# Moving the last batch's router chain, the row statistics and a hold on raw weights in a fused attention and mixture-of-experts kernel

## Chip, cores and metric

The kernel runs on one core of one Trainium2 chip. The metric is the device time of one execution in microseconds (us); lower is better. Engines are called as in the profile: PE (TensorE matmul, with PEld for its weight loads), DVE (VectorE), ACT (ScalarE), POOL (GpSimd) and SP (SyncE, which here only issues DMAs).

## What is computed

Causal attention with a cumulative bias (8 batches, 8 heads, 576 positions, head size 64), then a mixture of experts over the 4608 resulting rows of 512: each row goes to the one expert whose embedding it resembles most, passes through that expert's two layers and is scaled by the softmax weight of its choice.

```python
scores = scale * np.matmul(q, k.transpose(0, 1, 3, 2))
cum = np.cumsum(np.maximum(s, 0.0), axis=-1)
bias = -(cum[:, :, :, None] - cum[:, :, None, :])
scores = np.where(causal, -1000000000.0, scores + np.minimum(bias, 0.0))
...
out = np.matmul(attn, v)
...
logits = xn @ en.T / tau
expert_idx = np.argmax(logits, axis=1)
gate_w = probs[np.arange(N), expert_idx]
for e in range(E):
    mask = expert_idx == e
    h = np.maximum(x[mask] @ w1[e], 0.0)
    out[mask] = gate_w[mask, None] * (h @ w2[e])
```

## The kernel before, in words

The program is one instruction stream per engine, and its order is written out by hand (the schedule is manual): each engine takes its instructions in the order in which the program emits them, and waits at the head of its queue. So what sets the time around the change is who stands behind whom in a queue.

Attention runs head by head (`step(n)`, 64 heads). When the last head of a batch is normalised (`norm1` to `norm3`, which write the batch's rows into `xt`), `router` appends a chain of small tasks for that batch's 576 rows: `sume` (logits per expert, DVE), `sel1` to `sel5` (the largest one, as a one-hot `oh`), `rank0` (ten small PE matmuls that count rows per expert), `rank1` to `rank3` (DVE: the place `pos` of each row in its expert's list), and five scatters `scat` (indirect DMAs issued on POOL) that write the rows to the DRAM table `xs`. For the last batch, `rows` follows, which makes the indices of all later gathers. `chain(k)`, `slot`, `mslot` and `some` are the places at which the program takes tasks from this chain.

The experts run one after the other. Rows of an expert are gathered from `xs` by POOL in tiles of 128 (`xload(e, t)`, into one of three slots of `Qx`), transposed on PE (`xtr`), split into a high and a low half-precision part (`xcv`: high by ACT, low by DVE), and their statistics are taken (`xstat`: sum of squares by ACT, three small DVE operations). `gate` makes the row weights of them. Layer 1 (`l1`, line 903) computes for each of eight column blocks m twelve matmuls: four parts c times three products (high x high, high x low of the rows, low of the weights x high). ACT writes the high half of the result, DVE the low half (lines 909 and 910, called evacuation below). Layer 2 is `l2m` (line 974).

Expert 0 begins before its list is complete: while the last heads still run, its first 256 rows go through layer 1 (`first_pass(m)`, "pass m", between and after the last heads' `pv`), then its rows 256 to 383 (the third pass, `l1(m, 0, SPL, SPM)`), which need only the rows of earlier batches. Its row tiles 3 and 4 need the last batch's scatters: these are gathered by `xload(0, 3)` and `xload(0, 4)` and transposed in `third` and `fourth`, in the middle of layer 2 of tiles 1 and 2. `fifth` does row tile 2 of expert 1.

Weights come raw from DRAM through a ring of 14 places (`wissue`, DMAs of 128x512 floats on SP; tile number q counts them, 16 per expert), are squared and summed by ACT (`wsq`), scaled (`wparts`), and split: ACT writes the high half (`wcv`), DVE the low half (`wlow`, line 883, called low half below). When the low half of tile q is written, tile q + 15 is among those that may be issued; the DMA waits on SP for the place's last reader. Tiles 16 to 23 are layer 1 of expert 1, 24 to 31 its layer 2.

Around the change, after the last `pv`, one piece of the chain stands at a time between passes 1 to 7; `rank0` stands behind pass 5, `rank1` behind pass 7, `rank2`, `rank3`, `rows` and the scatters behind the third pass's first block, the low halves and statistics of row tiles 0 to 2 behind the whole third pass:

```python
first_pass(5)
some(0)
...
for m in range(8):
    l1(m, 0, SPL, SPM)
    if m == 0:
        some(4)
wlow(4)
classes()
for t in range(3):
    xstat(0, t)
    if t < 2:
        xload(0, t + 3)
```

Of the kernel before, what the change touches and what calls it, by code (L numbers as in the profile page):

```python
# [114 lines left out]
def main(ctx, tc, qkh, qkc, vtin, s_in, emb, tau, w1h, w2h, out, shared, nb):  # L115
# [573 lines left out]
    X, WT, HT = {}, {}, {}  # L689
# [80 lines left out]
    def xcv(e, t):  # L770
        pv = X[("p", e, t)].rearrange("p (c t) -> p c t", c=4)
        xH = X[("H", e)][:, :, 128 * t:128 * t + 128]
        nc.scalar.copy(xH, pv)
        xL = X[("L", e)]
        if isinstance(xL, tuple):
            xL = xL[e + t // (SPL // 128) > 0]
        nc.vector.tensor_tensor(xL[:, :, 128 * t:128 * t + 128], pv, xH, op=ALU.subtract)
# [102 lines left out]
    def wlow(k=99):  # L880
        for _ in range(min(k, len(lows))):
            q, l, a, s, h = lows.popleft()
            nc.vector.scalar_tensor_tensor(l, a, s, h, op0=ALU.mult, op1=ALU.subtract)  # L883
            wissue(q + 15)
# [6 lines left out]
    def l1(m, e, lo, hi, mid=None):  # L891
# [9 lines left out]
        for c in range(4):  # L901
            for k, (w, x) in enumerate(((wH, xH), (wH, xL), (wL, xH))):
                nc.tensor.matmul(h, w[:, 128 * c:128 * c + 128], x[:, c, lo:hi], start=(c == 0 and k == 0), stop=(c == 3 and k == 2))  # L903
                if m >= a0:
                    nc.tensor.matmul(X["a"][:, HALF * m:HALF * m + HALF], w[:, 128 * c:128 * c + 128], x[:, c, hi:hi + HALF], start=(c == 0 and k == 0), stop=(c == 3 and k == 2))  # L905
            if c == 1 and mid:
                mid()
# [279 lines left out]
    def step(n):  # L1187
# [43 lines left out]
        if n < NH:  # L1231
            wlow(1)
# [168 lines left out]
    for f in (norm1, norm2, norm3):  # L1401
        f(NH - 1)
        wn.pop(0)()
    wlow(1)
    first_pass(1)
    wn.pop(0)()
    chain(1)
    wn.pop(0)()
    wcv(2, True)
    first_pass(2)  # L1410
    chain(1)
    wlow(1)
    chain(2)
    wcv(2, True)
    first_pass(3)
    wcv(2, True)
    chain(1)
    wlow(1)
    chain(2)
    first_pass(4)  # L1420
# [3 lines left out]
    xcv(0, 2)  # L1424
    first_pass(5)
    some(0)
    wlow(1)
    wcv(1, True)
    xinfo(0, NF, NTL)
    first_pass(6)  # L1430
    wlow(1)
    wcv(1, True)
    first_pass(7)
    chain(1)
    wlow(1)
    wcv(1, True)
    for m in range(8):
        l1(m, 0, SPL, SPM)
        if m == 0:
            some(4)  # L1440
            assert not (mq or tasks or first or late or scats)
    wlow(4)
    classes()
    for t in range(3):
        xstat(0, t)
        if t < 2:
            xload(0, t + 3)
    for f in X[("g", 0, 0)][0:2]:
        f()
    xinfo(1, 0, NTL)  # L1450
    xload(1, 2)
# [254 lines left out]
```

## Time and profile before

| | |
|---|---|
| median of 3 runs | 764.95 us (763.99 to 767.49) |
| profiled execution | 763.98 us |
| its span, first to last instruction | 762.3 us |
| mean granted PE clock | 0.995 of full speed |
| PE, DVE, ACT, POOL busy | 97%, 70%, 75%, 52% of the span |

Times inside the profile count from the span's start. A row of the timeline gives the start, the duration, the engine, the line, what is written from what, and in brackets how long the engine stood idle before it and who ended that. Durations of matmuls overlap: the step from one start to the next is what one costs. The granted clock of PE is given in shares of full speed. Time that an engine other than PE stands idle costs nothing in itself.

### The profile page before, as it was taken

Reading aid. Unit: us, or ns where it says so; the run is one execution under the profiler, and the core shown is the slowest. Engines: PE = TensorE matmul, PEld = TensorE weight load, DVE = VectorE, ACT = ScalarE, POOL = GpSimd, SP = SyncE. Lnnn points to the kernel's source line nnn. Section 1 sums busy time; section 2 is a strip of 40 time slices with the busy share of each in tenths; the row PEclk is TensorE's granted clock in tenths of the full one; section 3 lists DMA queues with packets and bytes.
Section 4 is the critical chain, followed back from the end, with each engine's and each line's share of the span. In section 5 each row is a group of like instructions: output and inputs, shape, how many; then the busy total and the mean of one; then the engine's idle time right before and its main releaser. Section 6 shows DMA issues by size and latency. Waiting matters only on the chain. (4 is left out here: it accounts for less than half of the span.)

```text
span 762.3 us, 20951 instructions
## 1 busy us (share of the span) xinstructions
PE 739.1 (97%) x7992; PEld 536.4 (70%) x7992; DVE 530.2 (70%) x1818; ACT 568.2 (75%) x1029; POOL 397.2 (52%) x376
## 2 busy tenths in 40 slices
PE   7999999999999999999689999999999999999996
PEld 4889999999999999998365455545444554554554
DVE  8778888888888888898467767655665566745621
ACT  9898989898989998986377867837648578475410
POOL 9997898989897989693422113222221122312011
PEclk9999999999999999999899999999999999999999
DMA  7789879797979796874525956845755668553001
GB/s 151 175 193 191 173 180 204 180 207 168 216 172 210 181 215 155 174 256 132 172 89 168 207 171 194 159 139 152 181 171 141 177 186 186 169 130 100 13 15 58
DMA packets 76003, 124.01 MB, mean 163 GB/s; under 512 B 38824, under 2 KB 39232, under 8 KB 75033
## 3 DMA queue, kind: packets, MB, share of 16 engines
q0 software_dynamic: 19632, 69.69, 39.4%
q1 hardware_dynamic: 56260, 52.84, 25.9%
q8 instruction: 71, 1.16, 0.7%
q14 instruction: 40, 0.32, 0.1%
HBM read 93.99 MB, written 21.49 MB: 151 GB/s over the span
## 5 line engine op out<-in xcount | busy, mean ns | idle before, releaser
L252 POOL TENSOR_TENSOR PL<-P 128x576 f16<-128x576 f32 (+2 forms) x128 | 205.6, 1726 | 13.1 <-ACT P L498 8.6
L903 PE MATMUL pe<-xH,wt 128*128 128x512 f16 (+1 forms) x576 | 153.1, 344 | 0.5 <-PEq L1008 0.5
L982 POOL DMA_INDIRECT out<-Kx,xj x39 | 43.2, 1108 | 195.0 <-DVE Kx L981 164.5
L903 PEld LDWEIGHTS <-wt 128*128 128x128 f16 x960 | 86.0, 98 | 80.8 <-issue 1.5
L526 PE MATMUL om<-vh,P 128*128 128x73 f16 x960 | 106.9, 199 | 0.5 <-DVE sc L1035 0.3
L528 PE MATMUL om<-vh,PL 128*128 128x73 f16 x960 | 106.1, 197 | 0.9 <-POOL PL L252 0.9
L527 PE MATMUL om<-vl,P 128*128 128x72 f16 x960 | 106.3, 196 | 0.0
L739 POOL DMA_INDIRECT Qx<-xs,idx x40 | 46.5, 1163 | 108.3 <-ACT vjunk L838 41.3
L362 PE MATMUL s<-qkb 96*128 96x288 f32 (+4 forms) x272 | 96.2, 368 | 2.0 <-DVE M L370 0.9
L903 PE MATMUL pe<-xL,wt 128*128 128x512 f16 (+1 forms) x288 | 96.0, 344 | 0.0
L527 PEld LDWEIGHTS <-P 128*128 128x128 bf16 x960 | 94.7, 99 | 0.9 <-issue 0.5
L528 PEld LDWEIGHTS <-PL 128*128 128x128 f16 x960 | 93.8, 98 | 1.0 <-POOL PL L252 1.0
L526 PEld LDWEIGHTS <-P 128*128 128x128 bf16 x960 | 93.8, 99 | 0.6 <-DVE xt L551 0.4
L905 PE MATMUL pxs<-xH,wt 128*128 128x64 f16 x432 | 83.2, 193 | 0.0
L370 DVE CUSTOM_DVE_ANT_0 junk<-s,mS 128x448 bf16<-128x448 f32 (+3 forms) x144 | 73.9, 520 | 5.0 <-PE s L362 3.1
L974 PE MATMUL pxs<-wt,hq 128*128 128x512 f16 x297 | 74.0, 384 | 0.0
L501 ACT ACTIVATE P<-tb 128x1024 f32<-128x1024 f32 x64 | 65.2, 1018 | 3.0 <-PE tb L467 1.9
L974 PEld LDWEIGHTS <-hq 128*128 128x128 f16 x360 | 35.5, 99 | 42.7 <-issue 1.7
L905 PEld LDWEIGHTS <-wt 128*128 128x128 f16 x648 | 63.5, 98 | 0.4
L464 PE MATMUL tb<-QC,KC 128*128 128x448 f32 (+3 forms) x256 | 63.4, 307 | 0.0
L460 PE MATMUL tb<-qkb 128*128 128x448 f32 (+3 forms) x256 | 61.1, 286 | 0.0
L883 DVE SCALAR_TENSOR_TENSOR wt<-ring,idx,wt 128x512 f16<-128x512 f32 x80 | 56.8, 745 | 4.7 <-ACT wt L875 4.6
(328 smaller groups left out, 1997.3 us busy)
## 6 DMA issues: line engine op xcount, KB each, us to landing
qkb<-qkh POOLq DMA_DIRECT2D x15, 1216.0 KB, 8.9
ring<-w2h SPq DMA_DIRECT2D x44, 256.0 KB
ring<-w1h SPq DMA_DIRECT2D x36, 256.0 KB
KC<-qkh POOLq DMA_DIRECT2D x14, 576.0 KB, 8.5
QC<-qkh POOLq DMA_DIRECT2D x14, 576.0 KB, 9.1
vT<-vtin SPq DMA_DIRECT2D x24, 320.0 KB
rw<-w1h SPq DMA_DIRECT2D x15, 256.0 KB
rw<-w2h SPq DMA_DIRECT2D x12, 256.0 KB
```

The source lines that it names most:

```text
L252: nc.gpsimd.tensor_tensor(out, a, b_, op=ALU.subtract)
L362: nc.tensor.matmul(out, G[g]["QB"][0:96, h, 128 * i:128 * i + 128], G[g]["KB"][0:96, h, lo:hi], start=True, stop=True)
L370: nc.vector.tensor_tensor_reduce(out=jk, in0=src, in1=ms, scale=1.0, scalar=NEG, op0=ALU.add, op1=ALU.max, accum_out=MP[n // 2][:, n % 2, ...
L460: nc.tensor.matmul(out, G[g]["KB"][:, h, ks:ks + 128], G[g]["QB"][:, h, 64 + qlo:64 + qhi], start=start, stop=False)
L464: nc.tensor.matmul(out, HD[n]["KC"][:, ks:ks + 128], HD[n]["QC"][:, qlo:qhi], start=False, stop=stop)
L501: nc.scalar.activation(HD[n]["P32"][:, 576:1600], HD[n]["tb"], AF.Exp, scale=0.125)
L526: nc.tensor.matmul(out, lh, vh[:, kb], start=(kb == 0), stop=False)
L527: nc.tensor.matmul(out[:, u:u + 72], lh, vl[:, kb], start=False, stop=False)
L528: nc.tensor.matmul(out, ll, vh[:, kb], start=False, stop=(kb == j))
L903: nc.tensor.matmul(h, w[:, 128 * c:128 * c + 128], x[:, c, lo:hi], start=(c == 0 and k == 0), stop=(c == 3 and k == 2))
L905: nc.tensor.matmul(X["a"][:, HALF * m:HALF * m + HALF], w[:, 128 * c:128 * c + 128], x[:, c, hi:hi + HALF], start=(c == 0 and k == 0), sto ...
L974: nc.tensor.matmul(y, h, w, start=(m == 0 and k == 0), stop=(m == 7 and k == 2))
```

## The change

It moves work; no arithmetic is added but one memset of a single element. Four parts:

- The last batch's chain follows its rows at once: `sume` before pass 1, `sel1` to `sel5` in turn with the weight scaling behind pass 1, `rank0` inside pass 4 (behind its ninth matmul), `rank1` to `rank3` and the scatters behind pass 4. `rows` stands behind pass 6. High halves of weights (`wcv`) and the transposes of row tile 2 shift by a pass to make room, and one low half leaves the last head's step.
- Row statistics of tiles 0, 1 and 2 stand behind pass 7 and inside the third pass (behind blocks 1 and 4), each followed by the gather that takes its slot. Four low halves stand in the third pass as well.
- The order of matmuls inside `l1` for expert 0's first 256 rows and the first block of the third pass: products that need late operands come last.
- Raw weights from tile 22 on are held (`X["hold"]`) until a memset on POOL, behind the three gathers, has written into ring place 0; SP's DMA of tile 22 waits for it.

```diff
-    X, WT, HT = {}, {}, {}
+    X, WT, HT = {"hold": 22}, {}, {}
...
     def xcv(e, t):
+        xch(e, t)
+        xcl(e, t)
...
-            wissue(q + 15)
+            wissue(min(q + 15, X.get("hold", 16 * NE)))
...
-        for c in range(4):
-            for k, (w, x) in enumerate(((wH, xH), (wH, xL), (wL, xH))):
-                nc.tensor.matmul(h, w[:, 128 * c:128 * c + 128], x[:, c, lo:hi], start=(c == 0 and k == 0), stop=(c == 3 and k == 2))
...
-            if c == 1 and mid:
+        ps = [(wH, xH), (wH, xL), (wL, xH)]
+        if e == m == 0 and lo < SPM:
+            cs = [(c, p) for p in (ps[0], ps[2], ps[1]) for c in range(4)]
+        elif e + lo == 0:
+            cs = [(c, p) for c in range(4) for p in ps[0:2]] + [(c, ps[2]) for c in range(4)]
+        else:
+            cs = [(c, p) for c in range(4) for p in ps]
+        for i, (c, (w, x)) in enumerate(cs):
+            nc.tensor.matmul(h, w[:, 128 * c:128 * c + 128], x[:, c, lo:hi], start=(i == 0), stop=(i == 11))
...
+            if i == 8 and mid:
                 mid()
...
-        if n < NH:
+        if n < NH - 1:
             wlow(1)
...
     for f in (norm1, norm2, norm3):
         f(NH - 1)
-        wn.pop(0)()
-    wlow(1)
-    first_pass(1)
-    wn.pop(0)()
-    chain(1)
-    wn.pop(0)()
+    wlow(1)
+    chain(1)
+    first_pass(1)
+    for _ in range(5):
+        wn.pop(0)()
+        chain(1)
+    chain(1)
     wcv(2, True)
     first_pass(2)
-    chain(1)
-    wlow(1)
-    chain(2)
     wcv(2, True)
-    first_pass(3)
-    wcv(2, True)
-    chain(1)
     wlow(1)
-    chain(2)
-    first_pass(4)
+    first_pass(3)
+    l1(4, 0, 0, SPL, mslot)
+    chain(4)
+    some(0)
+    wcv(2, True)
+    wlow(1)
+    wcv(1, True)
+    first_pass(5)
     wlow(1)
     wcv(1, True)
     xtr(0, 2, pxs())
-    xcv(0, 2)
-    first_pass(5)
-    some(0)
-    wlow(1)
+    xch(0, 2)
+    first_pass(6)
+    xcl(0, 2)
+    chain(1)
     wcv(1, True)
     xinfo(0, NF, NTL)
-    first_pass(6)
-    wlow(1)
-    wcv(1, True)
     first_pass(7)
-    chain(1)
-    wlow(1)
+    xstat(0, 0)
+    xload(0, 3)
     wcv(1, True)
     for m in range(8):
         l1(m, 0, SPL, SPM)
         if m == 0:
-            some(4)
...
+        if m == 1:
+            xstat(0, 1)
+            xload(0, 4)
+        if m in (2, 3, 5, 6):
+            wlow(1)
+        if m == 4:
+            xstat(0, 2)
+            xinfo(1, 0, NTL)
+            xload(1, 2)
+            X.pop("hold")
+            nc.gpsimd.memset(HT["ring"][0:1, 0:1], 0.0)
+    wissue(14 + wdone[0] - len(lows))
     wlow(4)
...
     classes()
-    for t in range(3):
-        xstat(0, t)
-        if t < 2:
-            xload(0, t + 3)
-    for f in X[("g", 0, 0)][0:2]:
-        f()
-    xinfo(1, 0, NTL)
-    xload(1, 2)
```

`xch` and `xcl` are the two halves of the former `xcv`. The first two parts of `gate` run between `wlow(4)` and `classes()` now.

Order of DVE from the evacuations of passes 5 and 6 to the places, before (line 639 is `rank1`, 651 the end of `rank3` that writes `pos`, 910 an evacuation, 883 a weight low half, 777 the low part of row tile 2):

```order
L777 TENSOR_TENSOR xL<-pxs,xH 128x4x128
L910 SCALAR_TENSOR_TENSOR hq<-pxs,hq 128x256
L883 SCALAR_TENSOR_TENSOR wt<-ring,idx,wt 128x512
L910 SCALAR_TENSOR_TENSOR hv<-h,hv 128x256
L883 SCALAR_TENSOR_TENSOR wt<-ring,idx,wt 128x512
L910 SCALAR_TENSOR_TENSOR hv<-pxs,hv 128x256
L639 TENSOR_TENSOR idx<-om,base 128x40
L641 TENSOR_TENSOR base<-base,om 128x8
L883 SCALAR_TENSOR_TENSOR wt<-ring,idx,wt 128x512
L910 SCALAR_TENSOR_TENSOR hp<-pe,hp 128x128
L647 TENSOR_TENSOR idx<-idx,oh 128x40
L651 TENSOR_REDUCE pos<-idx 128x5
```

And in the change, from the choice (line 623, `oh`) to the places (922 is the evacuation, 889 the low half):

```order
L623 TENSOR_TENSOR oh<-wsel,idx 128x40
L922 SCALAR_TENSOR_TENSOR hq<-h,hq 128x256
L889 SCALAR_TENSOR_TENSOR wt<-wt,idx 128x512
L922 SCALAR_TENSOR_TENSOR hp<-pxs,hp 128x256
L922 SCALAR_TENSOR_TENSOR hq<-h,hq 128x256
L639 TENSOR_TENSOR idx<-om,base 128x40
L641 TENSOR_TENSOR base<-base,om 128x8
L647 TENSOR_TENSOR idx<-idx,oh 128x40
L651 TENSOR_REDUCE pos<-idx 128x5
```

Three evacuations (passes 2, 3 and 4) and one low half stand between choice and places now; the low halves of layer 2's weights and the evacuations of passes 5 to 7 have gone behind the places.

Order of PE at the rank matmuls (lines 630 to 636), in the change, inside pass 4 (line 915 is layer 1; `h` is pass 4's result):

```order
L915 MATMUL h<-rv,wt 128x256
L915 LDWEIGHTS wt
L915 MATMUL h<-xH,wt 128x256
L630 LDWEIGHTS tri
L630 MATMUL om<-oh,tri 128x40
L633 LDWEIGHTS onesb
L633 MATMUL om<-oh,onesb 128x32
```

Before, the same ten matmuls follow the last matmul of pass 5, one and a quarter passes later.

Order of POOL from the last batch's scatters (line 670) on, in the change, with line 739 the gathers and 1461 the memset:

```order
L713 MEMSET hq 128x64
L670 DMA xs<-xt,pos 36864x580 x5
L739 DMA Qx<-xs,idx 128x580 x3
L1461 MEMSET ring 1x1
L739 DMA Qx<-xs,idx 128x580
L994 DMA out<-Kx,xj 4608x512 x2
```

Only the memset is new on POOL; the three gathers ahead of it are tiles 3 and 4 of expert 0 and tile 2 of expert 1. SP's order is unchanged but for the wait of tile 22 on POOL.

## Rows read from the trace of the kernel before

**Rows 1.** The page's first part: busy time, share of the span, instructions, by engine.

```profile
PE 739.1 (97%) x7992; PEld 536.4 (70%) x7992; DVE 530.2 (70%) x1818; ACT 568.2 (75%) x1029; POOL 397.2 (52%) x376
```

**Rows 2.** Waits of PE from 355 to 500: total us, times, longest.

```profile
PE pxm L767 <- DMA Qx<-xs,idx: 5.9, 1, 5.9
PE pxs L767 <- DMA Qx<-xs,idx: 1.8, 1, 1.8
```

**Rows 3.** Timeline of PE around the first wait: start, us, operation, [idle before].

```profile
366.34 1.46 PE L974 MATMUL pxs<-wt,hp 128*128 128x512 f16 x6
367.64 0.81 PE L974 MATMUL pxs<-wt,hq 128*128 128x512 f16 x3
374.39 1.12 PE L767 MATMUL pxm<-ident,Qx 128*128 128x128 f32 x4 [5.94 <-DMA Qx<-xs,idx]
...
376.58 2.77 PE L974 MATMUL pxs<-wt,hq 128*128 128x512 f16 x6
```

**Rows 4.** Windows: us, busy of PE, PEld, DVE, ACT, POOL, PEclk, DMA share, GB/s.

```profile
355.00:361.00 6.00, 6.00 (x103) 5.91 (x102) 4.52 (x18) 3.56 (x11) 1.59 (x2) 1.00 0.49 161
361.00:368.50 7.50, 7.45 (x39) 3.30 (x36) 6.45 (x29) 4.39 (x14) 3.51 (x4) 1.00 0.80 270
368.50:374.40 5.90, 0.01 (x1) 0.01 (x1) 0.34 (x2) 0.00 (x0) 2.85 (x3) 0.86 0.31 104
374.40:380.00 5.60, 5.60 (x17) 2.60 (x18) 1.72 (x5) 2.65 (x7) 1.92 (x3) 0.54 0.43 104
...
395.80:402.00 6.20, 6.20 (x34) 3.35 (x35) 4.49 (x24) 4.82 (x13) 0.33 (x1) 1.00 0.20 59
```

**Rows 5.** Timeline of POOL: the last scatters of two batches, and the gathers behind them.

```profile
344.24 1.20 POOL L670 DMA_INDIRECT xs<-xt,pos  x1 [0.17 <-issue]
347.49 1.04 POOL L739 DMA_INDIRECT Qx<-xs,idx  x1 [2.05 <-DMA xs<-xt,pos]
...
359.10 1.02 POOL L670 DMA_INDIRECT xs<-xt,pos  x1 [10.00 <-DVE hp L910]
...
364.44 0.99 POOL L670 DMA_INDIRECT xs<-xt,pos  x1 [0.30 <-issue]
370.93 1.05 POOL L739 DMA_INDIRECT Qx<-xs,idx  x1 [5.50 <-DMA xs<-xt,pos]
```

**Rows 6.** Timeline of DVE: the last batch's rows, choice and places.

```profile
346.05 0.53 DVE L551 TENSOR_TENSOR xt<-om,z 128x360 f32<-128x360 f32 x1
...
351.43 0.19 DVE L623 TENSOR_TENSOR oh<-wsel,idx 128x40 bf16<-128x40 f32 x1
...
358.15 0.20 DVE L651 TENSOR_REDUCE pos<-idx 128x5 int32<-128x40 f32 x1
```

**Rows 7.** Timeline of PE: first matmul of pass 4, transposes of tile 2, rank matmuls.

```profile
349.35 0.27 PE L903 MATMUL h<-xH,wt 128*128 128x256 f16 x1
...
351.16 0.63 PE L767 MATMUL pxs<-ident,Qx 128*128 128x128 f32 x4 [0.34 <-DMA Qx<-xs,idx]
...
352.93 0.18 PE L630 MATMUL om<-oh,tri 128*128 128x40 bf16 x1
```

**Rows 8.** Timeline of DVE: low halves, and nine small statistics operations up to the reciprocal.

```profile
335.78 3.10 DVE L883 SCALAR_TENSOR_TENSOR wt<-rw,idx,wt 128x512 f16<-128x512 f32 x1
...
361.88 2.73 DVE L883 SCALAR_TENSOR_TENSOR wt<-ring,idx,wt 128x512 f16<-128x512 f32 x4
...
365.00 0.15 DVE L748 SCALAR_TENSOR_TENSOR xj<-Qx,idx 128x1 int32<-128x1 int32 x1
...
365.94 0.17 DVE L102 RECIPROCAL idx<-idx 128x3 f32<-128x3 f32 x1
```

**Rows 9.** Timeline of SP: weight loads beside the last scatters.

```profile
362.70 2.33 SPq L826 DMA_DIRECT2D ring<-w2h  x4
```

**Rows 10.** Timeline of ACT: one square of the row statistics with its read.

```profile
361.54 0.62 ACT L751 ACTIVATE vjunk<-Qx 128x512 bf16<-128x512 f32 x1
362.06 0.19 ACT L751 ACTIVATION_READ_ACCUMULATOR vjunk<-Qx 128x1 f32 x1
```

More of the change, by code (lines that the diff above doesn't have):

```diff
@@ L770, in xcv, with xch, xcl @@
     def xcv(e, t):
+        xch(e, t)
+        xcl(e, t)
+    def xch(e, t):
+        nc.scalar.copy(X[("H", e)][:, :, 128 * t:128 * t + 128], X[("p", e, t)].rearrange("p (c t) -> p c t", c=4))
+    def xcl(e, t):
         pv = X[("p", e, t)].rearrange("p (c t) -> p c t", c=4)
         xH = X[("H", e)][:, :, 128 * t:128 * t + 128]
-        nc.scalar.copy(xH, pv)
         xL = X[("L", e)]
@@ L900, in l1 @@
         h = (pe() if e or lo else pxs() if m % 2 else ps_t.tile([128, 2, 512], F32, tag="t", name="h")[:, 0])[:, 0:hi - lo]
-        for c in range(4):
-            for k, (w, x) in enumerate(((wH, xH), (wH, xL), (wL, xH))):
-                nc.tensor.matmul(h, w[:, 128 * c:128 * c + 128], x[:, c, lo:hi], start=(c == 0 and k == 0), stop=(c == 3 and k == 2))
-                if m >= a0:
-                    nc.tensor.matmul(X["a"][:, HALF * m:HALF * m + HALF], w[:, 128 * c:128 * c + 128], x[:, c, hi:hi + HALF], start=(c == 0 and k == 0), stop=(c == 3 and k == 2))
-            if c == 1 and mid:
+        ps = [(wH, xH), (wH, xL), (wL, xH)]
[7 more added lines that the diff above has]
+            nc.tensor.matmul(h, w[:, 128 * c:128 * c + 128], x[:, c, lo:hi], start=(i == 0), stop=(i == 11))
+            if m >= a0:
+                nc.tensor.matmul(X["a"][:, HALF * m:HALF * m + HALF], w[:, 128 * c:128 * c + 128], x[:, c, hi:hi + HALF], start=(i == 0), stop=(i == 11))
+            if i == 8 and mid:
                 mid()
@@ L1439, in main @@
         if m == 0:
-            some(4)
             assert not (mq or tasks or first or late or scats)
-    wlow(4)
-    classes()
-    for t in range(3):
-        xstat(0, t)
-        if t < 2:
-            xload(0, t + 3)
-    for f in X[("g", 0, 0)][0:2]:
-        f()
-    xinfo(1, 0, NTL)
-    xload(1, 2)
+        if m == 1:
[10 more added lines that the diff above has]
+    wissue(14 + wdone[0] - len(lows))
+    wlow(4)
+    g = X[("g", 0, 0)]
+    g[0]()
+    for i, f in enumerate(g[4]):
+        if i in (2, 5):
+            wlow(1)
+        f()
+    classes()
     def opening():
```

## The prediction, made before the change was run

> **What bounds the kernel now.** The page's first part comes first: TensorE (PE) is busy 97% of the span, VectorE (DVE) 70%, ScalarE (ACT) 75% [rows 1]. So only stretches in which PE stands still, or runs at the low clock, can be won. The list of waits of PE over the change between attention and experts has just two of weight, both for gathers of token rows: 5.9 and 1.8 us [rows 2]. The timeline shows the first: the second tile's output matmuls stop, and the transposes of row tile 3 of expert 0 begin at 374.39 after 5.94 us of nothing, so PE was free at 368.45 [rows 3]. The windows show what follows: after that standstill the granted clock is 0.54 in the stretch 374.4 to 380.0, about the lower of the two levels (1.2 against 2.4 GHz), where the stretches before and those after 395.8 show 1.00 [rows 4]. Six matmuls take 2.77 us there and 1.46 us at full clock [rows 3].
>
> Why that gather is late is read backwards. It was issued at 370.93, 5.50 us after POOL came free, and what ended that wait was the last scatter of rows landing; the five scatters of the last batch went out from 359.10 to 364.44 [rows 5]. The first scatter followed the places (`pos`), which DVE wrote at 358.15. The rows themselves were there at 346.05 + 0.53 = 346.58, and the one-hot choice `oh` at 351.43 [rows 6]. So 11.8 us lie between rows and places, and the work in them is short: what takes the time is the queue order, the rank matmuls standing behind pass 5 (352.93) [rows 7], and DVE's places standing behind weight halves and evacuations.
>
> **The change, part by part.**
>
> *Chain moved up.* DVE now does the row sums at about 347.2 (rows at 346.58, then one weight low half of 0.68, [rows 8]), and then the evacuation of pass 1 and eleven small operations, two chains interleaved. Nine such small operations took 365.94 - 365.00 = 0.94 us [rows 8]; dependent ones go slower, so I take 1.5 us, and `oh` at 349.5 instead of 351.43. The rank matmuls are now after the ninth of the 12 matmuls of pass 4, which starts at 349.35 [rows 7] and lasts 1.3 (its matmuls have half the columns of the 0.22 us ones below): they are due at 350.3, so PE does not wait for `oh`. If it did, the bound is the present time of `oh`, 351.6: 1.3 us. Next on DVE are the evacuation of pass 4 (PE ends it at 350.9, ACT 0.4 later, DVE at 351.8) and the four rank operations, so `pos` is there at 352.5 against 358.35. POOL followed 0.75 later [rows 5, 6]: the first scatter at about 353.2, 5.9 us earlier.
>
> *Scatters and gather.* Five scatters at (364.44 - 359.10) / 4 = 1.33 us: the last at 358.5. From the last scatter's issue to the gather that needs it took 370.93 - 364.44 = 6.5 us here, beside weight loads, and 347.49 - 344.24 = 3.25 us for the batch before [rows 5]. So the gather goes out between 361.8 and 365.0; I take nearer the first, because the loads beside the scatters go. From its issue to the transposes took 374.39 - 370.93 = 3.46 us [rows 3, 5]: rows in place at 365.2 to 368.5. PE wants them at 368.45. The wait of 5.94 us goes whole, or all but 0.1.
>
> *What the weight hold does.* Four loads of 256 KB were issued from 362.70 on [rows 9], where the DMA engines were 0.80 busy [rows 4]. Now tiles 22 to 29 go behind a one-element POOL memset that stands behind three gathers. POOL reaches it three issues of 1.33 after 361.8 to 365.0: at 365.8 to 369. Eight loads, 2.1 MB, at the 270 GB/s of the stretch 361.0 to 368.5 [rows 4] need 7.8 us, so they are in by 374 to 377. ACT asks for the first two of them (squares of tiles 22 and 23) behind the transposes of row tile 4. From 368.45 PE has 24 matmuls to do before those, at (367.64 - 366.34) / 6 = 0.22 [rows 3], and three groups of transposes of 0.6 [rows 7]: ACT asks at about 375.5, and waits 1.5 us at most. PE then has 15 more such matmuls (3.3), and two groups of 12 with a quarter of the columns (0.7 each) before its PSUM buffers are full and it needs ACT again: at about 381, with the branch between. Cost 0; the cover is PE's own work of that stretch. SP has nothing behind these loads that anyone asks for sooner.
>
> *Clock.* With no standstill the stretch 374.4 to 380.0 runs at 1.00: 5.60 x (1 - 0.54) = 2.6 us gained.
>
> *Row statistics in the third pass.* They leave a place where they cost PE nothing: it is busy 7.45 of 7.50 us there [rows 4]. In 355 to 361 DVE is busy 4.52 of 6 us, ACT 3.56 [rows 4]. DVE gets four low halves (2.73 [rows 8]) and three groups of statistics (0.94), and loses two low halves of 0.68 and the rank operations (0.8): 1.5 more, as much as is free. ACT gets three squares of 0.8 [rows 10], 2.4 more, again as much as is free. So both just keep up, and PE waits at most a little, for the late operand half of tile 2 in the first group of the third pass and a PSUM buffer of pass 7. Ends: 0, or the 1.5 in full behind PE. I take 0.4. The pass order that asks for the weights' low half last is the cover on DVE's late low halves; without it pass 6 would wait about 0.5.
>
> *Transposes of tile 2* now come after pass 5 instead of before it, so the 0.34 us they waited [rows 7] goes. The second large wait, 1.8 us, rests on a gather that goes out behind row tile 0 of expert 1 at the same distance as before: unchanged.
>
> *Sum:* -5.9 - 2.6 - 0.3 + 0.4 = -8.4 us. The profiled execution took 763.98 (span 762.3), so 755.6; the median of the three runs, 764.95, is 0.97 above it. On the median: **756.5 us**, -1.1%. About 0.5% (3.8 us) is what a measurement of this kernel can tell from no change.
>
> **A rule that speaks against it.** Scatters are now issued while DVE is densest. In the rows, 364.44 back to 359.10 were issued at even steps of 1.33, three of them while DVE did four low halves of two SBUF inputs in 2.73 us, 0.68 each: neither side slowed [rows 5, 8]. But one low half beside POOL's subtractions took 3.10 us [rows 8]. The Trainium skill, "SBUF — State Buffer", section "Who interferes with whom", has VectorE and GpSimd share a port pair under an exclusive lock, so that descriptors of a DMA issued on GpSimd wait for some VectorE operations. By that, scatters among DVE's copies and tensor_scalar work would come later than I take them (first rival); the trace bears out the lock for POOL's reading work, and for scatters not.
>
> **Rivals.**
> - *Scatters blocked or landing slowly.* As a mechanism of this kernel: if each of the five waited for one DVE operation, at most the 0.68 of a low half, the gather would be 3.4 us later, 365.2 to 368.4, and rows in place at 368.7 to 371.9: a wait of 0.3 to 3.4, up to about 760. For it: 6.5 us from the last scatter to the gather. Against: the even steps. This is also how the Trainium skill's rule of the port pair would show; no row shows a scatter held so. 10%.
> - *The wait only moves.* `oh` or the places come as late as before because DVE is bound, the wait stays above 4 us and the clock drops again: 761 to 764. Against: only small operations stand ahead of them. 4%.
> - *The 1.8 us wait goes as well,* because its gather meets less traffic: 756.5 - 1.8 = 754.7. Against: the moved loads have landed when that gather goes out, as before. 6%.
> - *The hold turns into a wait, and it is slower.* Place: ACT's squares of tiles 22 and 23, with evacuations behind them in its queue. If the eight loads run at the 104 GB/s seen from 368.5 to 380 [rows 4], they need 20 us and end at 386 to 389, against 381 where PE next needs ACT: a wait of 5 to 8, and 2.6 more for the clock. It eats the gain of 8.4 once they land after 387; at 389 the time is 764.95 + 8 + 2.6 - 8.4 = 767. For it: one burst of eight instead of spread loads, beside gathers. Against: 104 GB/s came with no work queued, and 270 with it. 3%.
>
> **How the numbers follow.** Forecast 77%, its own range 754.5 to 758.5 (0 to 1.5 us in the passes, and a median up to 1 us higher or lower, as runs lie). Chances: faster by over 0.5% is the forecast, the third rival and all of the first, with nothing of the rest counted: 0.93. Within 0.5%: 0.06, the second rival and the fourth up to a landing at 391. Slower: 0.01, the fourth beyond that. The range takes in the first and third rival: 753.8 to 760.0.
>
> **What would show it.** Right: in the list of PE's waits the 5.9 us entry for the gather is gone and the 1.8 us one stands; the granted clock is 1.00 from 361 to 400; the first scatter is at 353 to 354 and the gather 361.5 to 365.5; PE in 355 to 361 is without a wait over 0.5. Wrong: PE waits at the rank matmuls or in the third pass; the last scatter still takes over 7 us to release the gather; a wait of ACT on a ring load near 376 with PE standing still behind it; or a new standstill after 381.

## Result, and the profile after

The changed kernel takes 760.4 us (median of seven runs, 757.39 to 762.29). The kernel before, timed beside it, takes 766.47 (seven runs, 763.99 to 768.14). The ratio is 0.9914, with a 95% interval of 0.9897 to 0.993, so the change gains 6.6 us (5.4 to 7.9). The forecast was 756.5, a gain of 8.4. The profiled execution took 760.35 us, with a span of 758.6.

The kernels were timed in four sessions (the expectations say calls): the result; then the first four runs, the next four and the last four. The kernel before had medians of 766.47, 769.78, 766.38 and 769.53 us in them, so a ratio holds only inside its session. In the two sessions near 770 the profiles show PE standstills that have no releaser (such as 2.1 us in six pieces at L941, "<- issue"), and the one kernel that was timed in a session of each kind gained less there. What makes the difference is not shown; the third and the fourth session are both noted for the same chip.

Line numbers are shifted by the diff: of the lines cited, L767 stayed, L883 is L889, L903 is L915, L974 is L986. The waits of PE from 320 to 500 in the changed kernel (total us, times, longest; first three lines) answer to [rows 2]:

```profile
PE pxs L767 <- DMA Qx<-xs,idx: 3.0, 1, 3.0
PE om L526 <- DVE xt L551: 2.0, 1, 2.0
PE V L300 <- DVE vl L311: 0.5, 1, 0.5
```

The 5.9 us entry for `pxm` is gone. Its other gather wait grew from 1.8 to 3.0 us, and a wait of 2.0 for normalised rows (`om <- xt`) stands at 340, ahead of the stretch that the prediction looked at. The timeline of PE shows the three places: the wait at 340, the transposes of row tile 3, and the second gather wait with the six matmuls behind it [rows 3]:

```profile
340.31 0.19 PE L526 MATMUL om<-vh,P 128*128 128x73 f16 x1 [1.97 <-DVE xt L551]
...
370.40 0.60 PE L767 MATMUL pxm<-ident,Qx 128*128 128x128 f32 x4
...
390.36 1.12 PE L767 MATMUL pxs<-ident,Qx 128*128 128x128 f32 x4 [2.96 <-DMA Qx<-xs,idx]
391.34 2.54 PE L986 MATMUL pxs<-wt,hp 128*128 128x512 f16 x6
```

Row tile 3 starts without a wait, 3.99 us earlier than before. Behind the second wait six matmuls take 2.54 us, against 1.46 at full clock [rows 3]. The windows (columns as in [rows 4]) show the clock at 1.00 where it was 0.54 before, and a new low stretch from 387 to 395:

```profile
355.00:361.00 6.00, 5.82 (x79) 5.14 (x77) 4.72 (x20) 5.57 (x16) 4.39 (x5) 1.00 0.41 161
361.00:368.50 7.50, 7.50 (x69) 4.67 (x67) 7.33 (x22) 3.40 (x13) 4.16 (x5) 1.00 0.40 115
368.50:374.40 5.90, 5.90 (x33) 3.25 (x32) 3.33 (x16) 3.21 (x9) 0.91 (x1) 1.00 0.89 282
374.40:380.00 5.60, 5.60 (x30) 2.72 (x27) 2.72 (x9) 5.08 (x15) 1.44 (x3) 1.00 0.66 255
387.00:395.00 8.00, 5.04 (x25) 2.59 (x23) 3.93 (x25) 4.01 (x13) 1.76 (x2) 0.79 0.34 104
```

POOL's timeline has the scatters of the last batch, the gather of row tile 3, the memset that ends the hold, and at the end the out scatters (L994, which write finished rows to the output) and the gathers of row tiles 1 (380.95) and 3 (386.70) of expert 1 [rows 5]. The last is the one that the second wait is for; the expectations of the later runs call it row tile 1 in two places.

```profile
355.39 1.01 POOL L670 DMA_INDIRECT xs<-xt,pos  x1 [6.00 <-issue]
...
360.55 0.92 POOL L670 DMA_INDIRECT xs<-xt,pos  x1 [0.30 <-issue]
364.11 1.40 POOL L739 DMA_INDIRECT Qx<-xs,idx  x1 [2.64 <-ACT idx L87]
...
368.32 0.09 POOL L1461 MEMSET ring<- 1x1 f32 x1
...
379.66 0.99 POOL L994 DMA_INDIRECT out<-Kx,xj  x1 [3.86 <-DVE xj L79]
380.95 1.04 POOL L739 DMA_INDIRECT Qx<-xs,idx  x1 [0.30 <-issue]
385.41 0.99 POOL L994 DMA_INDIRECT out<-Kx,xj  x1 [3.42 <-PE pe L915]
386.70 1.04 POOL L739 DMA_INDIRECT Qx<-xs,idx  x1 [0.30 <-ACT xH L775]
```

The first scatter is 3.7 us earlier than before, not 5.9. The gather follows the last scatter's issue by 3.56 us, against 6.49. The second gather takes the slot of `Qx` that held row tile 0 of expert 1, and the last to read that slot is a DVE statistic (L79). Here are that statistic in the changed kernel, the same statistic before, and the gather behind it on POOL before:

```profile
384.33 0.27 DVE L79 TENSOR_REDUCE xj<-Qx 128x8 f32<-128x64 f32 x1
...
390.84 0.27 DVE L79 TENSOR_REDUCE xj<-Qx 128x8 f32<-128x64 f32 x1
...
392.00 1.04 POOL L739 DMA_INDIRECT Qx<-xs,idx  x1 [3.03 <-DVE hp L910]
```

Before, the gather went out 0.89 us after its slot had been read (391.11 to 392.00). In the changed kernel it went out 2.10 us after (384.60 to 386.70), since POOL was issuing the out scatter of 385.41 when the slot came free. That is 1.2 us more, and the wait grew by 1.1.

DVE's timeline shows why the scatters came later than forecast [rows 6, 8]:

```profile
334.24 0.79 DVE L508 TENSOR_TENSOR PL<-P 128x576 f16<-128x576 f32 x1
334.95 3.87 DVE L889 SCALAR_TENSOR_TENSOR wt<-rw,idx,wt 128x512 f16<-128x512 f32 x1
338.74 0.66 DVE L311 SCALAR_TENSOR_TENSOR vl<-V,sc,vh 128x432 f16<-128x432 f32 x1
...
339.73 0.53 DVE L551 TENSOR_TENSOR xt<-om,z 128x360 f32<-128x360 f32 x1
...
348.04 0.53 DVE L551 TENSOR_TENSOR xt<-om,z 128x360 f32<-128x360 f32 x1
...
351.27 0.19 DVE L623 TENSOR_TENSOR oh<-wsel,idx 128x40 bf16<-128x40 f32 x1
...
354.44 0.20 DVE L651 TENSOR_REDUCE pos<-idx 128x5 int32<-128x40 f32 x1
```

The chain itself is as short as forecast: from the end of the rows (348.57) to the places, 6.1 us instead of 11.8. It starts 2.0 us late, since a low half took 3.87 us at 334.95, ahead of the normalisation for which PE stood still at 340. Beside that low half POOL did a pair of subtractions, as POOL's timeline of the changed kernel shows:

```profile
335.24 3.02 POOL L252 TENSOR_TENSOR PL<-P 128x576 f16<-128x576 f32 x2
```

### The profile page after: what moved, and what is told of

It reads as the page before. It is cut to its first block, busy times and chain, and to the rows that moved or that the text cites. A ratio compares the mean times of both kernels' runs of the same rounds, so it can differ in the third digit from the quotient of the medians.

```text
span 758.6 us, 20953 instructions
## 1 busy us (share of the span) xinstructions
PE 738.8 (97%) x7992; PEld 536.2 (71%) x7992; DVE 531.3 (70%) x1818; ACT 567.7 (75%) x1029; POOL 396.7 (52%) x377
## 5 line engine op out<-in xcount | busy, mean ns | idle before, releaser
L915 PE MATMUL pe<-xH,wt 128*128 128x512 f16 (+1 forms) x576 | 153.0, 344 | 0.6 <-PEq L1020 0.5
L994 POOL DMA_INDIRECT out<-Kx,xj x39 | 43.0, 1103 | 201.6 <-DVE Kx L993 164.3
L915 PEld LDWEIGHTS <-wt 128*128 128x128 f16 x960 | 86.0, 98 | 81.6 <-issue 2.0
L915 PE MATMUL pe<-xL,wt 128*128 128x512 f16 (+1 forms) x288 | 95.6, 344 | 0.0
L986 PE MATMUL pxs<-wt,hq 128*128 128x512 f16 x297 | 72.7, 379 | 0.0
L986 PEld LDWEIGHTS <-hq 128*128 128x128 f16 x360 | 35.3, 98 | 42.0 <-ACT idx L88 0.3
L889 DVE SCALAR_TENSOR_TENSOR wt<-ring,idx,wt 128x512 f16<-128x512 f32 x80 | 56.8, 745 | 4.8 <-ACT wt L881 4.8
```

The source lines that it names most:

```text
L986: nc.tensor.matmul(y, h, w, start=(m == 0 and k == 0), stop=(m == 7 and k == 2))
```

## Experiments

Three questions were open. Which parts of the change make the gain? Is the 2.0 us wait the change's own, or the program's? Why did the second wait grow? All twelve runs follow, in the order of the sessions.

**No hold.** The whole change without the weight hold and the memset:

```diff
-    X, WT, HT = {"hold": 22}, {}, {}
+    X, WT, HT = {}, {}, {}
...
-            X.pop("hold")
-            nc.gpsimd.memset(HT["ring"][0:1, 0:1], 0.0)
```

> The changed kernel without the hold: weight tiles 22 to 29 are issued as their ring places come free, as before the change, beside the last scatters. Theory A (the hold's burst from 368.4 on slows the landing of the output scatters, and that holds the gather of tile 3 of expert 1 back on POOL): the output scatters go out less than 4.5 us apart, that gather goes out about 3.2 us behind the transposes of row tile 0 of expert 1 instead of 4.4, PE's second wait is back at 1.8 us or less instead of 3.0, and the clock stays at 1.00 behind it; in return the last scatter needs up to 6.5 us to release the first gather instead of 3.6, so the first gather goes out near 367 and PE waits 0 to 0.5 us there. Time about 757.5, 3 us below the changed kernel. Theory B (the hold is needed: without it the first gather comes late): PE waits over 2 us at the transposes of row tile 3, time 762 or more. Theory C (the hold does nothing to the time): 760 to 761, the second wait still near 3 us.

Measured: 766.89 us against 769.78, ratio 0.9964 (0.995 to 0.9978). The first gather wait is gone here too. On POOL the last scatter and the gather of row tile 3 stand as close as with the hold, 3.57 us apart:

```profile
362.29 0.92 POOL L670 DMA_INDIRECT xs<-xt,pos  x1 [0.30 <-issue]
365.86 1.51 POOL L739 DMA_INDIRECT Qx<-xs,idx  x1 [2.65 <-ACT hq L921]
```

So theory B, that the hold is needed for this, is out. SP issued the loads here only from 366.50 on, when that gather had gone out. The signs that theory A named came too: out scatters 3.8 us apart, the second gather 3.17 us behind the transposes of row tile 0, a second wait of 2.0, and the clock at 1.00 behind it. The gain that it forecast can't be read here: no kernel that differs by the hold alone was timed in the second session, and the next run, which has the hold, overlaps this one.

**Out scatters declared independent of each other:**

```diff
+        for p in outs:
+            tc.declare_no_dep(ins, p, reason="each row of the output belongs to one row of one tile")
+        outs.append(ins)
```

> The changed kernel, but each output scatter no longer waits for the landing of the one before (they write different rows). Theory A (POOL's queue stands behind those landings, and the gather of tile 3 of expert 1 with it): that gather goes out about 3.2 us behind the transposes of row tile 0 of expert 1, PE's second wait falls from 3.0 to 1.8 us or less, the clock does not drop behind it; time about 757.5. Rival (the gather is late for its own landing or because of the row statistics on ACT and DVE): POOL idles no longer before the output scatters, but the second wait stays near 3 us and the time at 760.

Measured: 767.62, ratio 0.9977 (0.9965 to 0.9989), no faster than without the hold. The out scatters moved (378.46, 380.41, 385.09), and the second gather went out at 388.95, 0.90 us after the slot's last reader and no longer behind an out scatter. The wait was 2.1 and the clock stayed at 1.00. So an out scatter makes up only a part of the wait; the rest is the distance from the slot's last reader to the transposes.

**Earlier row tile.** Row tile 0 of expert 1 is prepared, and row tile 3 gathered, in layer 2 of tile 2, ahead of the out scatter:

```diff
+    def sixth():
+        xprep(1, 0, pxm())
+        xload(1, 3)
-    l2(0, 2, {2: fourth, 7: l1t})
+    l2(0, 2, {2: fourth, 5: sixth, 7: l1t})
...
-            if e == 0 and m in (1, 5):
-                xprep(1, m // 4, pxm())
-                xload(1, 3 + m // 4)
+            if e == 0 and m == 5:
+                xprep(1, 1, pxm())
+                xload(1, 4)
```

> The changed kernel, but row tile 0 of expert 1 is transposed behind block 5 of layer 2 of row tile 2, 3.5 us of PE time earlier, and the gather of tile 3 of expert 1, which takes its slot in Qx, follows it at once, ahead of the output scatter. If the second wait is only the distance between these two points, it goes whole: no wait over 0.5 us from 361 to 402, clock 1.00 throughout, time 755 to 756.5 (760.4 less 3.0 of wait and 1.7 of half clock). If the gather's row data are not there that early, or another wait takes its place (the next gather, tile 4): gain under 2 us.

Measured: 766.24, ratio 0.9951 (0.9936 to 0.9965), the lowest of its session, though its interval overlaps that of the version without the hold. No gather wait is left in PE's list. A new one of 1.5 us took part of its place ("PE pe L962 <- issue").

**Chain alone.** The chain and the order of the matmuls as in the change, but statistics and gathers behind the whole third pass, and no hold:

```diff
-    X, WT, HT = {"hold": 22}, {}, {}
+    X, WT, HT = {}, {}, {}
...
-        if m == 1:
-            xstat(0, 1)
-            xload(0, 4)
...
+    classes()
+    for t in range(3):
+        xstat(0, t)
+        if t < 2:
+            xload(0, t + 3)
...
```

> Only the chain is moved up (with the order of matmuls in the passes): row statistics and the three gathers stand behind the third pass as before, and there is no hold. Theory A (the chain alone takes away the first wait; statistics and hold are cover): the last scatter is issued near 360.5, the first gather goes out at 364 to 367, bound by the scatters' landing, PE waits 0 to 0.5 us at row tile 3, and with the weights loaded early the second wait is 1.8 us: about 757.5. Rival (the statistics must move as well, since the gather waits for the slot that they read): the first gather goes out over 2 us behind the last landing, and PE waits over 1.5 us at row tile 3: 760 or more.

Measured: 769.94, ratio 1.0002 (0.9992 to 1.0011): nothing gained. POOL's timeline shows the last scatter, and the gather of row tile 3 10.8 us behind it:

```profile
361.92 0.92 POOL L670 DMA_INDIRECT xs<-xt,pos  x1 [0.30 <-issue]
372.69 1.06 POOL L739 DMA_INDIRECT Qx<-xs,idx  x1 [9.86 <-DVE idx L102]
```

DVE's timeline of the same run has the low halves, and the last operation of the first and of the third row statistic behind them:

```profile
368.41 2.73 DVE L889 SCALAR_TENSOR_TENSOR wt<-ring,idx,wt 128x512 f16<-128x512 f32 x4
...
371.66 0.26 DVE L79 TENSOR_REDUCE xj<-Qx 128x8 f32<-128x64 f32 x1
...
372.28 0.26 DVE L79 TENSOR_REDUCE xj<-Qx 128x8 f32<-128x64 f32 x1
```

The gather writes the slot of `Qx` that the first statistic reads, and that one stands behind four low halves on DVE. The gather goes out 0.77 us after it has ended (371.92 to 372.69), as the first scatter goes out 0.75 us after the places have [rows 5, 6]; by then the scatters had long been issued. So the gather is bound by the slot's reader here. PE waits 2.9 us for it, half of the 5.9 before, with the clock at 0.55 to 0.60 behind that wait. Yet no time is gained. No profile of the kernel before was taken in the second session, so why is not known. The version without the hold, which differs from this one only in the place of the statistics, the gathers and the gate's operations, had 0.9964 in the same session.

**The kernel before, once more,** unchanged, for a second profile.

> The kernel before once more, for a second profile of it. In all five changed kernels so far PE waits 2.0 us for the normalised rows (om <- xt), behind a weight low half that began just before POOL's pair of subtractions and took 3.87 us; the one profile of the kernel before has no such wait (its low half took 0.74 there, 1.6 us before the pair). The order of instructions on DVE and POOL is the same in both up to that place. Theory A, chance of phase: a weight load that lands half a microsecond earlier or later decides who goes first, and the kernel before falls into the same collision in most of its executions; then this profile has the wait of about 2.0 us and a low half of over 3 us ahead of the normalisation, and a span about 2 us longer than its other parts explain. Theory B, the change makes the phase: then this profile has no PE wait over 0.5 us on xt between 325 and 345.

Measured: 764.31, theory A. The waits of PE from 320 to 500 in this second execution of the kernel before:

```profile
PE pxm L767 <- DMA Qx<-xs,idx: 5.6, 1, 5.6
PE om L526 <- DVE xt L551: 2.0, 1, 2.0
PE pxs L767 <- DMA Qx<-xs,idx: 1.7, 1, 1.7
```

Its DVE timeline, from a weight statistic that waited for a load to the low half:

```profile
321.93 1.14 DVE L835 CUSTOM_DVE_ANT_0 junk<-vh 128x512 bf16<-128x512 f32 x1 [0.41 <-DMA vh<-w1h]
...
325.11 1.53 DVE L508 TENSOR_TENSOR PL<-P 128x576 f16<-128x576 f32 x1
...
334.73 3.87 DVE L883 SCALAR_TENSOR_TENSOR wt<-rw,idx,wt 128x512 f16<-128x512 f32 x1
```

So the slow low half and its wait belong to the program, not to the change. In the first profile of before the same DVE instructions read:

```profile
322.37 0.71 DVE L835 CUSTOM_DVE_ANT_0 junk<-vh 128x512 bf16<-128x512 f32 x1 [0.84 <-DMA vh<-w1h]
...
325.13 0.74 DVE L508 TENSOR_TENSOR PL<-P 128x576 f16<-128x576 f32 x1
...
333.68 0.74 DVE L883 SCALAR_TENSOR_TENSOR wt<-rw,idx,wt 128x512 f16<-128x512 f32 x1
```

That execution is where DVE waited longest for that load, and it is the only one of the seven profiles up to here in which the low half was over before POOL's pair began. The two profiles of before differ by 1.8 us in this wait (0.18 and 1.97) and by only 0.33 us in time (763.98, 764.31). The rows show where the second nearly makes it up: the first has a PE wait of 0.9 us for POOL at 344.13 that the second lacks, and the second has 0.3 us less at the first gather wait, 0.6 less of low clock behind it, and 0.2 less at the second.

**The whole change, once more,** in the same session.

> The whole change once more, beside the others of this call and on their chip. If the gain is the change's and not one chip's, the ratio is 0.990 to 0.995, and the profile has again no gather wait at the transposes of row tile 3, one of about 3 us at those of row tile 1 of expert 1 with the granted clock under 0.9 behind it, and the 2.0 us wait for xt. If the hold costs nothing and gives nothing, it stands with the kernel without the hold (0.9964 on another call); if the hold is needed, it is clearly below that.

Measured: 761.32 against 766.38, ratio 0.9937 (0.9913 to 0.9962), as expected. The waits are 2.0 (xt) and 2.6 (second gather), and the clock is 0.52 and 0.63 in 390 to 392 and 392 to 394. The gather of row tile 3 of expert 1 again stands behind an out scatter (384.30) and goes out 1.35 us after its slot was read. Beside the second profile of before, the spans are 757.9 against 762.6. No version without the hold ran in the third session, so it says nothing on the hold's worth.

**Low half behind the normalisation.** The whole change, with the low half that collides moved behind the normalisation of the next step:

```diff
         norm3(n - 3)
+        if n == NH - 1:
+            wlow(1)
...
-        if n < NH - 1:
+        if n < NH - 2:
             wlow(1)
```

> The whole change, but the low half of the step before last goes behind the normalisation of the step after it instead of ahead of it, so that a low half that meets POOL's pair of subtractions holds up nobody. If the 2.0 us wait for xt is that collision, it goes (under 0.5 us left), the router chain of the last batch starts about 2 us earlier, and the kernel is 2 us faster than the whole change in the same call, ratio about 0.0026 lower. If the wait is something else (PE ahead of DVE for another reason), it stays at 1.5 us or more. If PE's time there was covered later on, the wait goes and the time stays.

Measured: 756.69 us, ratio 0.9879 (0.9855 to 0.9903), 4.6 us below the whole change in its session. DVE's timeline has the low half slow again, now behind the normalised rows, and the chain 2 us earlier:

```profile
336.47 0.53 DVE L551 TENSOR_TENSOR xt<-om,z 128x360 f32<-128x360 f32 x1
336.92 1.88 DVE L889 SCALAR_TENSOR_TENSOR wt<-rw,idx,wt 128x512 f16<-128x512 f32 x1
...
349.18 0.19 DVE L623 TENSOR_TENSOR oh<-wsel,idx 128x40 bf16<-128x40 f32 x1
...
352.36 0.20 DVE L651 TENSOR_REDUCE pos<-idx 128x5 int32<-128x40 f32 x1
```

POOL's timeline then has every time that the prediction named:

```profile
353.31 1.01 POOL L670 DMA_INDIRECT xs<-xt,pos  x1 [3.42 <-DVE wt L889]
...
358.48 0.92 POOL L670 DMA_INDIRECT xs<-xt,pos  x1 [0.30 <-issue]
362.03 1.40 POOL L739 DMA_INDIRECT Qx<-xs,idx  x1 [2.64 <-ACT idx L87]
```

The 2.0 us wait is gone, which is 2.0 of the 3.7 us between the two spans (757.9 and 754.2). The other 1.7 is the clock: it stays at 1.00 from 380 to 396, though PE has the same second wait (2.61 against 2.55). PE's work from these transposes to the next ones takes 5.70 us here, and 7.37 in the whole change beside it.

**Both: the low half and the earlier row tile.**

> Low half behind the normalisation, and the preparation and gather of row tile 0 of expert 1 one out scatter earlier, on top of the whole change. The two losses read from the profile of the changed kernel are 2.0 us (xt) and 3.0 us with about 1.5 us of low clock behind it (second gather). If both are real and add up: no PE wait over 1.6 us from 325 to 500, and 4 to 6 us faster than the whole change in the same call. If the second is only exchanged for waits on something else: within 2.5 us of it.

Measured: 754.35, ratio 0.9848 (0.982 to 0.9876), the fastest of all and 7.0 us below the whole change in its session, more than the 4 to 6 expected. The waits of PE from 320 to 500, the longest three:

```profile
PE pe L962 <- ACT vjunk L751: 1.3, 1, 1.3
PE V L300 <- DVE vl L311: 0.4, 1, 0.4
PE om L526 <- DVE base L641: 0.3, 1, 0.3
```

The 2.6 us gather wait has become 1.3 us for ACT, which is busy with squares and their reads from 369.71 to 378.6 there, with gaps of 0.3 us for two splits of rows.

**Statistics alone.** The kernel before, with only the statistics and the issue of the gathers moved into the third pass:

```diff
+        if m in (1, 3):
+            xstat(0, m // 2)
+            xload(0, 3 + m // 2)
+        if m == 5:
+            xstat(0, 2)
     wlow(4)
     classes()
-    for t in range(3):
-        xstat(0, t)
-        if t < 2:
-            xload(0, t + 3)
```

> The kernel before, with the row statistics and the issue of the gathers moved into the third pass, and neither the chain nor the hold. If the places and the scatters set the gather of row tile 3, as the prediction has it, nothing is gained: the first scatter stays at 359 to 361, the gather at 370 to 372.5, the wait of PE at 5 to 6 us, ratio 0.998 to 1.002. If the late statistics alone held that gather (as the chain-only kernel suggests, whose gather stood behind them), the gather goes out earlier by over 2 us and the ratio is below 0.996.

Measured: 769.29, ratio 0.9996 (0.9981 to 1.0011): nothing gained. The scatters came no earlier (361.83 to 366.99). The gather went out 3.57 us behind the last of them, at 370.56, so here the data bind it and not the slot. Its wait was 1.4 instead of the 5 to 6 expected, but PE had already stood 3.4 us for low halves, which came late behind the third pass ("PE pxs L974 <- DVE wt L883: 3.4").

**The low half behind the normalisation, in the kernel before** (the same move, with `n < NH and n != NH - 2` in its condition):

> The kernel before, with the low half of the step before last behind the normalisation of the step after it, as in the kernel that was 4.6 us faster than the whole change. If the collision costs the kernel before as much, the wait for xt goes and the ratio is 0.994 to 0.997. If the kernel before takes it back further down (the gather waits end with it either way, since its second profile, with the 2.0 us wait, took no longer than the first without it), the wait goes and the ratio is 0.998 to 1.002.

Measured: 768.45, ratio 0.9987 (0.9972 to 1.0002), no gain that can be told. The profile does not settle it: a wait for `xt` of 1.6 us stands there for another reason, shown with the last run. It also has a wait of 2.6 us for low halves ahead of the first gather wait, which is 0.8 us here, though nothing was moved there. So the waits around that gather lie otherwise in the fourth session than in the profile that the forecast was made from, and what the chain or the statistics alone are worth where that wait is 5.6 to 5.9 us was not measured.

**Low half moved, no hold,** and **low half moved, with hold, once more** in the same session:

> The whole change with the low half behind the normalisation, and without the hold of the raw weights and the memset that ends it. If the hold neither costs nor gives, it stands within 1.5 us of the same kernel with the hold in this call, and the gather of row tile 3 again goes out about 3.6 us behind the last scatter's issue. If the hold is what makes the scatters land in 3.6 us, the gather goes out later by over 1.5 us, and a wait of PE returns at row tile 3. If the held burst is what makes the second gather late, the second wait falls to under 2 us and the kernel is 1 to 2.5 us faster than with the hold.

> The whole change with the low half behind the normalisation once more, as the partner of the kernel without the hold and to see whether its gain stands: ratio 0.986 to 0.990, no wait for xt over 0.5 us, no gather wait at row tile 3, one of 2 to 3 us at row tile 1 of expert 1. If the earlier gain of 4.6 us over the whole change was chance of that chip, the ratio is over 0.991.

Measured: 766.21, ratio 0.9948 (0.9932 to 0.9965), without the hold; 764.66, ratio 0.9941 (0.9926 to 0.9957), with it. The intervals overlap and the medians are 1.5 us apart, so a worth of the hold can't be told from nothing. The second wait is 2.0 in both, and in both the second gather goes out 0.89 us after its slot was read, with no out scatter in its way. So the held burst does not make the wait longer here. Whether it is what delays the out scatters in the other sessions stays open: the last two ahead of that gather are 5.75, 4.66 and 4.75 us apart in the three profiles in which one of them held it up, all with the hold, and 3.80 and 3.70 in the two versions of the change without it; but they are 3.84 in this second kernel, which has the hold, and 4.68 and 4.21 in the kernel before, which has none. The last scatter is followed by the gather 3.57 and 3.55 us later.

The second kernel missed its expectation: 0.9941 instead of 0.986 to 0.990, and a wait for `xt` of 1.6 us. It is not the slow low half, which took 1.88 us behind the normalised rows. DVE's timeline of that run:

```profile
337.47 1.88 DVE L889 SCALAR_TENSOR_TENSOR wt<-rw,idx,wt 128x512 f16<-128x512 f32 x1
341.98 0.17 DVE L539 TENSOR_SCALAR z<-om 128x5 f32<-128x5 f32 x1 [2.64 <-PE pxs L767]
```

DVE was done at 339.35 and waited 2.64 us for PE, where it waited 1.07 in the first run of this kernel. PE's recorded rows are alike in both up to there, so PE's signal came late for a reason that no row shows. The kernel before with the same move has this standstill there too (1.6 us). The gain of 4.6 us over the whole change was seen in one session alone.

## Why the prediction was right, and where its sizes were off

- **First wait, -5.9: right.** It went whole, by the mechanism named: early scatters, and a gather soon behind them. What the prediction did not say is that the gather needs its slot of `Qx` as well. It booked the statistics only as a cost of 0.4 ("they leave a place where they cost PE nothing"), while they are what frees the slot in time: with the chain alone POOL stood idle for 9.86 us and the gather followed the slot's reader. The chain alone gave 1.0002, against 0.9964 with the statistics moved too and no hold; the statistics alone gave 0.9996 in another session.
- **Clock behind it, -2.6: right.** The stretch 374.4 to 380.0 went from 0.54 to 1.00. The step from row tile 3's transposes to row tile 4's, 5.59 us before and 3.02 in the changed kernel, says the same. **Transposes of tile 2, -0.3: right,** they start without a wait.
- **"The first scatter at about 353.2, 5.9 us earlier": 3.7 in the changed kernel.** The step that failed here is the start of the sum, "the rows were there at 346.58", taken from an execution in which a low half happened to miss POOL's subtractions. In the other profile of before, in the statistics-alone kernel and in the six profiles of the change and its parts that leave that low half in its place, it took 3.87 us ahead of the normalisation. With it moved, `oh`, `pos`, the first and the last scatter came at 349.18, 352.36, 353.31 and 358.48, against 349.5, 352.5, 353.2 and 358.5 named. The late start did not cost the gain, as PE was 2.0 us late with it and the gather wait still went whole. That the time was then 756.69, beside 756.5 forecast, is partly luck: that kernel has a second wait of 2.61 us where the forecast has 1.8, and had a ratio of 0.9941 in another session.
- **"From the last scatter's issue" 3.25 to 6.5 us, taken near the first: right,** 3.56. Kernels with four loads issued beside the last scatters had 6.49 and 6.26; without them it is 3.55 to 3.69 in every profile whose statistics stand in the third pass. For that the order of issue was enough; the hold was not needed.
- **"The second large wait ... unchanged": wrong,** and the largest miss of the sum. The wait was 2.96 and 2.55 in the two profiles of the change, against 1.83 and 1.66 before. The gather was said to go out "at the same distance" behind row tile 0 of expert 1. From that tile's transposes to the gather it was 3.17 us before, and 4.37 and 3.63 in the change, since an out scatter stood ahead of it on POOL when its slot came free. Where none did, the wait was 1.7 to 2.1, before and in the variants; where the gather went ahead of that out scatter altogether, it was gone. Why the out scatters of the change come later is open. Behind the wait the clock fell to 0.54 and 0.61 (390 to 394), a term the sum does not have: from these transposes to the next ones PE took 7.24 us, against 5.70 in runs whose clock stayed at 1.00, so 1.5 us. Not every wait there is followed by it (see the end), so this term is in part the luck of one execution.
- **Sum over profiles.** Against the second profile of before, with the same 2.0 us wait: -5.6 for the first wait, -2.0 for the clock behind it (4.97 us from transposes to transposes against 3.02), +0.2 in the passes, +1.3 for the second wait, +1.5 for the clock behind that: -4.6, where the span of 762.6 became 758.6, -4.0. The other 0.6 us is not placed. The medians differ by 6.1 us and the ratio gives 6.6: both profiled executions of before (763.98, 764.31) lie 2 us or more below the medians of their sessions, while the one of the change lies at its median. The forecast stood on 764.95, from three runs; with the ratio that makes 758.4, within its range of 753.8 to 760.0, though the median of 760.4 itself is just above it. In the second session with the whole change the granted clock over the span was 0.989 to 0.995 in the eleven runs of before, and 0.993 to 0.996 in its own six.
- **Hold, 0: right as a cost.** ACT came to the squares of the held tiles at 378.37 and did not wait. **Third pass, +0.4:** no wait of PE over 0.5 in 355 to 361 (5.82 of 6.00 busy); from the normalised rows to row tile 3's transposes PE took 30.09 us, against 29.87 in the second profile of before, so +0.2.
- **The rule of the port pair.** The Trainium skill, "SBUF — State Buffer", "Who interferes with whom", has a DMA's descriptors from GpSimd wait for some VectorE operations. The runs do not show it for scatters: with the low half moved, five issues came at (358.48 - 353.31) / 4 = 1.29 us while DVE was busy 3.99 of these 5.17 us. But that was mostly two-operand work and reductions, not the copies and `tensor_scalar` operations of which the prediction spoke, so this rival was hardly tested. For POOL's subtractions the low half shows the cost, 0.74 to 3.87 us, and the prediction had seen it at 3.10 [rows 8] without asking what would happen ahead of a normalisation.

Left open: why the clock fell behind some second waits and not behind others; what holds PE in the sessions near 770; whether the hold is worth anything or delays the out scatters; why the chain alone gained nothing though its wait was shorter; and the 0.6 us.

## What to carry to other kernels

A wait for a gather has several conditions: its data in place, its slot read to the end, and its own turn in the queue of the engine that issues it. Moving one of the first two gained nothing here (1.0002 and 0.9996), and the third made the second wait longer; list them all before pricing one. Take the start of a sum from two profiles if one operation in it stands beside a competing engine: a low half that began 1.62 us ahead of POOL's pair of subtractions took 0.74 us, and one that began 0.28 us ahead took 3.87. Work that nobody needs may be worth moving behind what others wait for: moving that one low half gained 4.6 us on the changed kernel in one session, while on the kernel before, in another, no gain could be told (0.9987).

## What was not expected of the hardware

- A low half on DVE that met POOL's pair of subtractions at 335 ended 0.55 to 0.57 us behind the pair, wherever it had begun: 3.87 us long when it began 0.28 or 0.29 us ahead of the pair, 3.10 and 1.88 us long when it began inside it. Clear of the pair it took 0.74. This is no rule of the engines: in the first profile of before, one beside the pair ahead of that (POOL 329.74 to 332.60) began at 330.17, took 1.64 us and ended before the pair did. A DVE subtraction (L508) likewise took 1.53 us beside POOL's work and 0.74 without. In the two profiles of before, what differs ahead of this is a weight statistic 13 us earlier that waited 0.84 or 0.41 us for its load and then took 0.71 or 1.14; that this set who met whom was not tested.
- The length of a PE wait alone did not decide whether the granted clock fell behind it. At the second gather it fell behind six waits of 1.88 to 2.96 us, to 0.50 to 0.54 for some 2 us, and stayed at 1.00 behind six of 1.66 to 2.61 us; 2.55 and 2.61 went different ways (0.53 and 1.00).
- The same kernel before took 766.4 us in two sessions and 769.6 in two others, and the gain of one change differed between them (0.9879 and 0.9941).
